# Blocks of one and two chunks, units of one chunk by two batches, and a mixture's first product in tiles of 64 rows

## The chip, the cores and the metric

One core of one Trainium2 chip, all in 32-bit floats. The metric is the time of one execution on the device in microseconds (us), as the median of several executions. Executions fall into a fast and, now and then, a slow state. A ratio is the mean time of one kernel's fast runs over that of the kernel before's fast runs in the same rounds on the same chip, so it isn't quite the ratio of the medians that stand beside it.

Words used throughout: TensorE multiplies matrices, VectorE and ScalarE work elementwise, SyncE and GpSimd here mostly start transfers (DMA). The *clock* is the share of full speed that TensorE was granted, as its profile records it. Names like `pef` or `ph` are those of the tiles that TensorE writes. *Filler* is mixture work that TensorE does while the recurrence waits for something. A *half* is a matmul of the first mixture product with 64 rows instead of 128; two halves on different rows of the array can run at the same time and are then a *pair*.

## The reference

A recurrence over 768 tokens for 4 batches of 8 heads, then a mixture of four experts over all 3072 tokens.

```python
# r, k, v, w, a, b: (4, 8, 768, 40); state: (B, H, 40, 40)
for t in range(S):
    y[:, :, t] = einsum('bhd,bhde->bhe', r_t, state)
    Sa = einsum('bhde,bhe->bhd', state, a_t)
    state = state * w_t[..., None] - einsum('bhd,bhe->bhde', Sa, b_t) + einsum('bhd,bhe->bhde', v_t, k_t)
x = y.transpose(0, 2, 1, 3).reshape(3072, 320)
for e in range(4):                       # w1[e]: 320 x 1024, w2[e]: 1024 x 320
    out += p[:, e:e + 1] * (np.maximum(x @ w1[e], 0) @ w2[e])
```

## The kernel before

The recurrence goes in chunks of 64 tokens. Within a chunk it is a triangular system. It is solved on VectorE's lanes for all heads at once. A block is two chunks of all four batches, and a *unit* is one batch of it. For each block the kernel prepares four units (transposes `pW`, `pNK`, `pKN`, `pA`, `pR`; VectorE's scan, reciprocal and products; `pef`; `pkn`), sends the systems F through DRAM to VectorE's lanes, solves, brings the result back, completes the inverse (`pi`, `px`), and does two dependent steps (`pa` to `py`).

```python
for tb in range(NT):                      # six blocks of 128 tokens
    pairs = [pair(tb, bp) for bp in range(NP)]
    decays(pairs[0], 0)                   # load of W, pW, scan, reciprocal
    for bb in range(B):
        if bb + 1 < B:
            decays(pairs[(bb + 1) // 2], (bb + 1) % 2)
        within(pairs[bb // 2], bb % 2)    # pNK, pKN, pA, pef, pkn, pR
        if bb % 2:
            to_lanes(pairs[bb // 2])      # F -> DRAM -> lanes
    solve()                               # VectorE
    for q in pairs:
        inverse(q)                        # pi, px
    ...                                   # two steps, gather into xT
    if before is not None:
        mixture(tb - 1, before, gate)     # one block behind
    before = xT
mixture(NT - 1, before, gate)
```

The mixture's first product multiplies a depth of 320: two tiles of 128 rows (`w1a`), and one of 64 rows (`w1c`), in which two output tiles run at once.

```python
for f2 in range(NF // 2):
    ph = [mbank("ph") for _ in range(2)]
    for x in ((0, 1) if f2 % 2 == 0 else (1, 0)):
        for d in range(2):
            if x == 1:                    # 64 rows, a pair
                nc.tensor.matmul(out=ph[d][:], lhsT=w1c[half(d), f2, :], rhs=xv[half(d), 2, :], ...)
                continue
            for g in range(2):            # 128 rows
                nc.tensor.matmul(out=ph[d][:], lhsT=w1a[:, g, f * P:(f + 1) * P], rhs=xv[:, g, :], ...)
    ...                                   # relu to hs, on ScalarE
for bb in range(B):
    ...                                   # po: eight 128-row matmuls, scaled and added into osb on VectorE
```

The program states what depends on what. The order of the instructions on each engine is fixed when the kernel is built, by a scheduler that estimates durations: it takes the earliest written instruction that it believes ready. The mixture is written after the recurrence, so it is filler.

Of the kernel before, what the change touches and what calls it, by code (L numbers as in the profile page):

```python
# [14 lines left out]
def kernel(  # L15
# [29 lines left out]

    nc = tc.nc
# [6 lines left out]
    NT = S // P  # L53
    NJ = H // 2
    NP = B // 2
    SL = (0, 64)
    NF = F // P
    NTOK = B * S
# [7 lines left out]

    def bank(name):
        return ps.tile([P, 512], FP32, name=name, tag="bank", bufs=4)
# [4 lines left out]

    ident = const.tile([P, P], FP32, name="ident")
    nc.vector.memset(ident[:], 1.0)
# [3 lines left out]
    )  # L79

    upper = const.tile([P, P], FP32, name="upper")
    nc.vector.memset(upper[:], 1.0)
# [7 lines left out]

    first = const.tile([P, 2 * NJ, L + 1], FP32, name="first")
    nc.vector.memset(first[:], 0.0)
    nc.vector.memset(first[:, :, 0:1], 1.0)



    srcs = {"W": (w, w), "NK": (b, k), "KN": (k, b), "A": (a, a), "R": (r, r)}
    nat = {x: const.tile([P, H, 64], FP32, name=f"nat{x}") for x in srcs}
    for x in srcs:
        nc.vector.memset(nat[x][:, :, D:64], 1.0 if x == "W" else 0.0)  # L100
    w_shift = const.tile([P, 2 * NJ, L + 1], FP32, name="w_shift")
    nc.vector.memset(w_shift[:, :, 0:1], 0.0)
    RV = [const.tile([P, 2, NJ, 2, 64], FP32, name=f"RV{p}_") for p in range(NP)]
    VS = [const.tile([P, 2, NJ, 2, 64], FP32, name=f"VS{p}_") for p in range(NP)]
    XT = [const.tile([P, 2, 2 * NJ, L], FP32, name=f"XT{p}_") for p in range(NP)]
# [12 lines left out]

    def gates():

        gate = const.tile([P, NTOK // P, E], FP32, name="gate")
        total = const.tile([P, NTOK // P], FP32, name="total")
        nc.gpsimd.dma_start(out=gate[:], in_=moe_domain_probs.rearrange("(n p) e -> p n e", p=P))
        nc.vector.reduce_sum(out=total[:], in_=gate[:], axis=AX.X)
        nc.vector.tensor_scalar_add(out=total[:], in0=total[:], scalar1=1e-9)
        nc.vector.reciprocal(out=total[:], in_=total[:])
        nc.vector.tensor_mul(gate[:], gate[:], total[:, :, None].to_broadcast([P, NTOK // P, E]))
        return gate
# [7 lines left out]
    def load(x, tb, bb):  # L136
        t = slice(tb * P, (tb + 1) * P)
        if srcs[x][0] is srcs[x][1]:
            nc.sync.dma_start(out=nat[x][:, :, 0:D], in_=srcs[x][0][bb, :, t, :].rearrange("h t e -> t h e"))
            return  # L140
        for s in range(2):
            nc.sync.dma_start(
                out=nat[x][:].rearrange("p (j s) e -> p j s e", s=2)[:, :, s, 0:D],
                in_=srcs[x][s][bb].rearrange("(j s) t e -> s t j e", s=2)[s, t],
            )
# [11 lines left out]
    class Pair:  # L157
        pass

    def pair(tb, bp):  # L160
        q = Pair()
        q.GI = []
        q.tb, q.bp = tb, bp
        q.G = sb.tile([P, 2, 2 * NJ, L + 1], FP32, name="G", tag="G", bufs=2)
        q.AE = sb.tile([P, 2, 2, 2, NJ, L], FP32, name="AE", tag="AE", bufs=2)
        q.KN = sb.tile([P, 2, 2, NJ, 2, D], FP32, name="KN", tag="KN", bufs=2)
        q.F = sb.tile([P, 2, 2, NJ, L], FP32, name="F", tag="F", bufs=2)
        q.R = sb.tile([P, 2, NJ, P], FP32, name="R", tag="R", bufs=2)
        return q

    def decays(q, i):

        load("W", q.tb, 2 * q.bp + i)
        G = q.G[:, i]
        nc.scalar.copy(
            out=w_shift[:, :, 1:L + 1], in_=turn("W")[:].rearrange("p (c t) -> p c t", t=L),
        )
        nc.vector.tensor_tensor_scan(
            out=G.rearrange("p c t -> p (c t)"), data0=w_shift[:].rearrange("p c t -> p (c t)"),
            data1=first[:].rearrange("p c t -> p (c t)"), initial=0.0, op0=ALU.mult, op1=ALU.add,  # L180
        )
        GI = sb.tile([P, 2 * NJ, L], FP32, name="GI", tag="GI", bufs=2)
        nc.vector.reciprocal(out=GI[:], in_=G[:, :, 1:L + 1])  # L183
        q.GI.append(GI)

    def within(q, i):

        G, GI = q.G[:, i], q.GI[i]
        for x in ("NK", "KN", "A", "R"):
            load(x, q.tb, 2 * q.bp + i)  # L190
        KNT = sb.tile([P, 2 * NJ, 2, L], FP32, name="KNT", tag="KNT", bufs=1)
        for x, name in enumerate(("NK", "KN")):
            nc.vector.tensor_tensor(
                out=KNT[:, :, x, :], in0=turn(name)[:].rearrange("p (m t) -> p m t", t=L), in1=GI[:], op=ALU.mult,
            )
        pa = turn("A")
        for s in range(2):
            nc.vector.tensor_tensor(  # L198
                out=q.AE[half(s), i, s], op=ALU.mult,
                in0=pa[half(s)].rearrange("p (j c t) -> p c j t", j=NJ, c=2),  # L200
                in1=G[half(s), :, 0:L].rearrange("p (j c) t -> p c j t", c=2),
            )

        pef = [bank("pef") for _ in range(2)]
        for c in range(2):
            for j in range(NJ):
                for s in range(2):
# [44 lines left out]
    def square(t, n=Q):  # L252

        return t[:, 0:Q * Q].rearrange("p (a c) -> p a c", c=Q)
# [344 lines left out]
```

## Time and profile before

| | us |
|---|---|
| median of 3 runs | 1418.68 (1415.52 to 1424.13) |
| until the first unit of the second block | 162.6 |
| second block | 235.7 |
| a steady block (blocks 3 to 5) | 219.5 to 221.4 |
| one expert alone | 35.2 |

A block can be read as a sum: its four stages (preparing, waiting for the solve, inverse, steps), in which the recurrence sets the pace and filler is free, and whatever mixture is then left, alone. Before, the stages are 160 us and 59.7 us are left. The lines are in the prediction.

### The profile page before, as it was taken

To read this page: it belongs to the slowest core of one execution; us is meant where nothing else is said; L and a number is where in the kernel's file an instruction comes from. 1 tells how busy PE (TensorE), PEld (TensorE's weight loads), DVE (VectorE), ACT (ScalarE), POOL (GpSimd) and SP (SyncE) were. 2 spreads that over 40 slices of the span, in tenths; PEclk is the share of its full clock that TensorE was granted. 3 is DMA by queue.
4 is the path that set the end of the run, shared out by engine and by line. 5 is a ranking of instruction groups with operands and counts; after the bars stand their busy time and mean duration, and the time that the engine had idled before them with its cause. 6 is when DMAs were issued, how large, how long until landed. Compare 5 with 4: busy or idle time off the path is not lost.

```text
span 1422.5 us, 24433 instructions
## 1 busy us (share of the span) xinstructions
PE 1307.6 (92%) x10592; PEld 870.4 (61%) x10592; DVE 557.3 (39%) x806; ACT 262.0 (18%) x481; POOL 182.7 (13%) x331
## 2 busy tenths in 40 slices
PE   4608899899999999999999999999999999999998
PEld 3608766576557567566568556558555657655555
DVE  8373656232054824045715035625125544200000
ACT  1202131121122131112121113112012213011111
POOL 4000001101201201201200221010220120222220
PEclk8556889999998999999999998999998999999999
DMA  9612454433257433248343356453335342222221
GB/s 147 92 32 42 82 73 101 89 74 81 79 98 113 103 81 80 76 97 122 86 98 62 85 116 93 83 125 60 95 103 74 90 105 62 59 93 76 74 77 50
DMA packets 294217, 121.98 MB, mean 86 GB/s; under 512 B 267184, under 2 KB 277984, under 8 KB 294112
## 3 DMA queue, kind: packets, MB, share of 16 engines
q1 hardware_dynamic: 273696, 57.44, 24.7%
q0 software_dynamic: 20416, 62.99, 16.0%
q8 instruction: 84, 1.38, 0.4%
q14 instruction: 21, 0.17, 0.0%
HBM read 103.07 MB, written 17.30 MB: 85 GB/s over the span
## 4 chain that ended last, share of the span: by engine, by line
PE 74%; DVE 20%; DMA 4%; issue 2%; SPq 0%; ACT 0%; DVEq 0%
PE po L528 24%; PE ph L518 17%; PE ph L511 5%; DVE tmp L279 5%; PE pef L208 5%; DVE GI L183 3%; PE pc L414 3%; PE pkn L226 2%; DVE Xl L283 2%; DVE Y L283 2%; DMA XD<-Tl 2%; PE py L430 2%; PE pa L360 2%; PE py L440 2%; PE pSN L461 2%; PE pt L375 2%
## 5 line engine op out<-in xcount | busy, mean ns | idle before, releaser
L528 PE MATMUL po<-w2s,hs 128*128 128x320 f32 x1536 | 430.9, 438 | 0.0
L528 PEld LDWEIGHTS po<-w2s,hs 128*128 128x128 f32 x1536 | 292.7, 192 | 127.6 <-issue 16.2
L518 PE MATMUL ph<-xT,w1a 128*128 128x512 f32 x768 | 361.2, 610 | 1.5 <-DMA xT<-yD 1.5
L518 PEld LDWEIGHTS ph<-xT,w1a 128*128 128x128 f32 x768 | 139.9, 192 | 172.6 <-issue 168.7
L536 DVE SCALAR_TENSOR_TENSOR osb<-po,gate,osb 128x320 f32<-128x320 f32 x72 | 39.6, 551 | 463.3 <-PE po L528 463.3
L524 ACT ACTIVATE hs<-ph 128x512 f32<-128x512 f32 x192 | 109.6, 596 | 587.0 <-PE ph L511 439.6
L499 POOL DMA_DIRECT2D w1c<-in_moe_w_dram x96 | 53.3, 562 | 794.9 <-PE ph L511 791.2
L511 PE MATMUL ph<-xT,w1c 64*128 64x512 f32 x384 | 111.2, 633 | 0.0
L208 PE MATMUL pef<-AE,KNT 64*128 64x64 f32 x768 | 70.6, 310 | 31.5 <-DVE AE L198 31.5
L208 PEld LDWEIGHTS pef<-AE,KNT 64*128 64x128 f32 x768 | 66.8, 221 | 45.8 <-issue 34.9
L183 DVE RECIPROCAL GI<-G 128x512 f32<-128x512 f32 x24 | 80.3, 3345 | 0.2
L495 POOL DMA_DIRECT2D w1a<-in_moe_w_dram x144 | 74.3, 522 | 39.5 <-PE ph L518 32.5
L321 PE MATMUL pi<-F 32*32 32x32 f32 x768 | 18.7, 199 | 56.8 <-DMA F<-XD 56.8
L511 PEld LDWEIGHTS ph<-xT,w1c 64*128 64x128 f32 x384 | 36.0, 189 | 55.7 <-issue 54.7
L503 POOL DMA_DIRECT2D w2s<-in_moe_w_dram x24 | 22.1, 921 | 366.0 <-PE po L528 365.9
L218 DVE TENSOR_TENSOR AE<-pef,mask 64x512 f32<-64x512 f32 x48 | 33.1, 689 | 72.8 <-ACT F L214 72.0
L467 DVE COPY SN<-pSN 128x512 f32<-128x512 f32 x24 | 16.6, 692 | 109.8 <-PE pSN L461 109.8
L321 PEld LDWEIGHTS pi<-F 32*32 32x32 f32 x768 | 16.1, 115 | 69.2 <-issue 67.4
L414 PE MATMUL pc<-R,VST 64*128 64x64 f32 x768 | 48.5, 276 | 6.0 <-DVE VST L467 5.6
L414 PEld LDWEIGHTS pc<-R,VST 64*128 64x128 f32 x768 | 45.2, 188 | 14.2 <-DVE VST L467 7.1
L214 ACT COPY F<-pef 64x512 f32<-64x512 f32 x48 | 27.8, 580 | 120.3 <-PE pef L208 119.8
L279 DVE TENSOR_TENSOR tmp<-Xl,Gl 128x256 f32<-128x256 f32 (+3 forms) x36 | 45.6, 1266 | 0.6
(108 smaller groups left out, 1134.9 us busy)
## 6 DMA issues: line engine op xcount, KB each, us to landing
w2s<-in_moe_w_dram POOLq DMA_DIRECT2D x24, 1280.0 KB, 7.4
w1a<-in_moe_w_dram POOLq DMA_DIRECT2D x144, 160.0 KB, 3.9
w1c<-in_moe_w_dram POOLq DMA_DIRECT2D x96, 64.0 KB, 2.3
natW<-in_w_dram SPq DMA_DIRECT2D x24, 160.0 KB
natA<-in_a_dram SPq DMA_DIRECT2D x24, 160.0 KB
natR<-in_r_dram SPq DMA_DIRECT2D x24, 160.0 KB
yD<-Yo SPq DMA_DIRECT2D x48, 80.0 KB
out_dram<-osb SPq DMA_DIRECT2D x24, 160.0 KB
```

What stands on the lines that cost most here:

```text
L183: nc.vector.reciprocal(out=GI[:], in_=G[:, :, 1:L + 1])
L208: nc.tensor.matmul(out=pef[s][:, (c * NJ + j) * L:(c * NJ + j + 1) * L], lhsT=KNT[half(s), 2 * j + c].rearrange("p x t -> p (x t)"), rhs=q ...
L279: nc.vector.tensor_tensor(out=m, in0=in0[:, :, None, :].to_broadcast([P, n0, n1, nr]), in1=in1[:, None, :, :].to_broadcast([P, n0, n1, nr] ...
L283: nc.vector.tensor_reduce(out=out, in_=m, axis=AX.X, op=ALU.add, negate=negate)
L414: nc.tensor.matmul(out=pc[s][:, at], lhsT=VST[half(s), i, j * P:(j + 1) * P], rhs=q.R[half(s), i, j, c * L:(c + 1) * L], start=True, stop= ...
L495: nc.gpsimd.dma_start(out=w1a[j * D:(j + 1) * D, s, :], in_=moe_w1[e, h * D:(h + 1) * D, :])
L499: nc.gpsimd.dma_start(out=w1c[SL[d] + s * KR:SL[d] + (s + 1) * KR], in_=moe_w1[e, h * D + P - K0:(h + 1) * D, :].rearrange("r (f d x) -> r ...
L511: nc.tensor.matmul(out=ph[d][:], lhsT=w1c[half(d), f2, :], rhs=xv[half(d), 2, :], start=(f2 % 2 == 1), stop=(f2 % 2 == 0),)
L518: nc.tensor.matmul(out=ph[d][:], lhsT=w1a[:, g, f * P:(f + 1) * P], rhs=xv[:, g, :], start=(f2 % 2 == 0 and g == 0), stop=(f2 % 2 == 1 and ...
L524: nc.scalar.activation(out=hs[-1][:], in_=ph[d][:], func=ACTF.Relu)
L528: nc.tensor.matmul(out=po[:, 0:DM], lhsT=hs[f][:, bb * P:(bb + 1) * P], rhs=w2s[:, f, :], start=(f == 0), stop=(f == NF - 1),)
L536: nc.vector.scalar_tensor_tensor(out=osb[bb][:], in0=po[:, 0:DM], scalar=sc, in1=osb[bb][:], op0=ALU.mult, op1=ALU.add,)
```

## The change

Its intent: a first block of one chunk, so that the mixture begins sooner, and a last block of one chunk, so that little mixture is left at the end; units of one chunk by two batches, which suit both block sizes; and a first product made of pairs alone, with fewer changes of the array's tiling. The diff, cut to its core (renaming, loads, buffers and constants left out):

```diff
-    for tb in range(NT):
-        pairs = [pair(tb, bp) for bp in range(NP)]
+    blocks_of = [[0]] + [[c, c + 1] for c in range(1, NC - 1, 2)] + [[NC - 1]]
+    for cs in blocks_of:
+        units = [Of(c=c, x=x, p=p, ...) for x, c in enumerate(cs) for p in range(NP)]
 ...
     def load(x, u):
-        nc.sync.dma_start(out=nat[x][:, :, 0:D], in_=srcs[x][0][bb, :, t, :]...)
+        for i in range(2):
+            nc.sync.dma_start(out=nat[x][half(i)][:, :, 0:D], in_=...)
 ...
-            w1a = wts.tile([P, 2, F], FP32, name="w1a", tag="w1a", bufs=1)
-            w1c = wts.tile([P, NF // 2, P], FP32, name="w1c", tag="w1c", bufs=1)
+            w1s = wts.tile([P, NK, F // 2], FP32, name="w1s", tag="w1s", bufs=1)
 ...
-                for x in ((0, 1) if f2 % 2 == 0 else (1, 0)):
+                for k_ in range(NK):
                     for d in range(2):
-                        if x == 1:
-                            nc.tensor.matmul(... w1c[half(d), f2, :] ...)
-                            continue
-                        for g in range(2):
-                            nc.tensor.matmul(... w1a[:, g, f * P:(f + 1) * P] ...)
+                        nc.tensor.matmul(
+                            out=ph[d][:, 0:n], lhsT=w1s[half(d), k_, f * P:(f + 1) * P], rhs=xT[half(d), k_, 0:n],
+                            start=(k_ == 0), stop=(k_ == NK - 1),
+                        )
 ...
-            nc.sync.dma_start(out=out[row:row + P, :], in_=osb[bb][:])
+            for i in range(2):
+                nc.sync.dma_start(out=out[row:row + L, :], in_=osb[tt][half(i)])
```

## The prediction

> **What bounds the kernel now.** I read the page first (busy shares, the 40 slices), then the chain of waits, then the busy time in chosen stretches, then TensorE's timeline through one block, then its waits. The kernel has two halves: a recurrence over chunks of 64 tokens and, one block behind it, a mixture of four experts (first product `ph`, second product `po`) that fills TensorE while the recurrence waits.
>
> ```profile
> PE 1307.6 (92%) x10592; PEld 870.4 (61%) x10592; DVE 557.3 (39%) x806; ACT 262.0 (18%) x481; POOL 182.7 (13%) x331
> PE   4608899899999999999999999999999999999998
> PEclk8556889999998999999999998999998999999999
> ```
>
> TensorE is busy nearly everywhere but in the first four slices (36 us each), where it is idle or at a granted clock near half. One steady block (398 to 618 us), cut at its own stages (preparing the units; waiting for the triangular solve; inverse; two steps; mixture alone):
>
> ```profile
> 398.00:453.00 55.00, 52.02 (x302) 35.44 (x301) 33.56 (x33) 16.10 (x31) 7.20 (x13) 0.88 0.73 118
> 453.00:498.80 45.80, 43.16 (x145) 24.89 (x144) 30.48 (x52) 5.34 (x10) 7.23 (x13) 1.00 0.41 98
> 498.80:517.20 18.40, 18.40 (x238) 10.31 (x238) 1.10 (x2) 4.53 (x8) 0.93 (x1) 1.00 0.46 112
> 517.20:558.20 41.00, 40.05 (x904) 35.15 (x903) 22.31 (x39) 10.52 (x21) 0.00 (x0) 1.00 0.29 54
> 558.20:618.00 59.80, 59.80 (x201) 34.57 (x198) 4.55 (x8) 6.84 (x12) 13.45 (x25) 1.00 0.31 85
> ```
>
> The columns are length, then busy us of PE, PEld, DVE, ACT, POOL, then clock, DMA share, GB/s. The first four stages, 160 us, are the recurrence; 60 us are mixture alone. So a block is 220 us. What matters is the second stage. From TensorE's timeline there:
>
> ```profile
> 449.07 2.33 PE L208 MATMUL pef<-AE,KNT 64*128 64x64 f32 x32
> 451.34 1.09 PE L226 MATMUL pkn<-ident,KNT 128*128 128x128 f32 x8
> 453.24 13.62 PE L528 MATMUL po<-w2s,hs 128*128 128x320 f32 x50
> 466.70 3.60 PE L518 MATMUL ph<-xT,w1a 128*128 128x512 f32 x8
> 470.23 1.99 PE L511 MATMUL ph<-xT,w1c 64*128 64x512 f32 x8
> 472.15 7.13 PE L518 MATMUL ph<-xT,w1a 128*128 128x512 f32 x16
> 484.67 11.47 PE L528 MATMUL po<-w2s,hs 128*128 128x320 f32 x42
> 498.77 0.22 PE L321 MATMUL pi<-F 32*32 32x32 f32 x2 [2.64 <-DMA F<-XD]
> ```
>
> From the last `pef` (ends at 451.3) to the first `pi` are 47.4 us: F through DRAM to the lanes, the solve on VectorE, the result back through DRAM. TensorE has just enough mixture in that gap and waits only 2.64 us. The same wait in the whole run, and the path's other two ends:
>
> ```profile
> PE pi L321 <- DMA F<-XD: 56.8, 8, 40.0
> 456.07 0.48 SPq L243 DMA_DIRECT2D Gl<-FD  x1
> 463.07 0.15 DVE L267 TENSOR_TENSOR tmp<-Xl,Gl 128x4 f32<-128x4 f32 x1
> 491.60 0.46 SPq L307 DMA_DIRECT2D XD<-Xl  x1
> ```
>
> 40 us of the wait belong to the first block, which has no mixture. In the first block the solve starts 3.5 us after the issue of Gl (67.93 to 71.39); here it starts after 7.0, since an eviction of `po` stands ahead of it in VectorE's order.
>
> **What the skill says.** Trainium skill, "TensorE: Matmul & The Clock Gate", Part 2: matmuls stay in program order, only weight loads are pulled ahead. So TensorE's built order is fixed, and filler placed after `pi` can't move ahead of it. The trace agrees: it idles 2.64 us before `pi` although `po` matmuls stand right behind.
> Same page, Part 3: matmuls of different row groups run at the same time. The trace agrees: each f32 matmul of the program is two records; the eight 64-row records at 470.23 take 1.92 us until 472.15, while the sixteen 128-row ones take 7.06, so 441 ns each. Eight in pairs are four slots of 427 ns and 0.2 us over.
> "TensorEngine Tiling (Array Packing)", Key Properties: a change of tiling mode drains the array. The trace agrees as to size: that 0.2 us over, and 0.1 to 0.2 at each run of 128-row records beside them.
> First page, Part 1: idling beyond a window of some 3.4 us halves the clock. The trace agrees: after 2 us of waiting at 409 us the clock falls to 0.60 in 412 to 416 us, and it stays near 0.5 from 427 to 436, with small matmuls alone.
>
> **The change part by part.**
> *First product in 64-row tiles.* Before, per expert: 16 full matmuls and 8 half ones, 1278.16 to 1296.12 in the chain of waits, 17.96 us; `po` takes 17.23 (35.2 together). After: 40 half matmuls, two by two, 20 pairs of two slots of 427 ns, 17.1 us, and one entry and exit, 0.3: 17.4. The array does the same work; four mode changes become two. Gain 0.5 us per expert, with 24 experts' worth about 10 us. The count of instructions is 40 for 24.
> *Blocks of 1, 2, 2, 2, 2, 2, 1 chunks.* Seven solves for six. A solve runs on all lanes at once, so half the lanes make it no shorter. The short ends cost two half mixtures of about 17.6 us an expert. Prologue: only two of four units are prepared. The last `pef` then ends near 34.8 instead of 63.7 us (the second unit's group starts at 34.40 and takes 4.37, less 4 for the third unit's scan and reciprocal, 1.2 and 3.3, which no longer stand between): 29 off. One step of 19.6 us off; the half inverse 3 off; 1 on for a split dot product. So 162.6 us (the first transpose of the next block) less 50.6 is 112.
> *Units of one chunk by two batches.* The same transposes, `pef`, `pkn` and steps. Loads become two half-size DMAs each; 18 issues per unit at 0.5 us are 9 us of SyncE, under a unit's 12 to 14 us. Gathers read whole kilobyte rows. Neutral.
> *What the order does.* This is the part that decides it. The instruction order of the changed kernel shows what fills each gap. Between last `pef` and first `pi` of a steady block: `pkn`, one `ph`, `pR`, 6 `ph`, 32 `po`, 26 `ph`. Costs: 1.0, 1.05 (alone: two slots and mode changes), 0.44, 2.8, 17.3, 11.3 (13 pairs): 33.9 us. Before it was 45. The order looks as if a half matmul had been counted at 0.86 us: 33 x 0.86 + 17.2 + 1.4 is 47, just the length of the path. In pairs they take half of that, so the filler runs out.
> The path itself: 47.4, less 3.5 (the solve no longer stands behind evictions), plus 1.65 (three more evictions of 0.55 inside it), plus 0.6 (two products of 2048 split): 46.1. So TensorE idles 46.1 - 33.9, about 12 us, before each `pi`, and 2 us more are lost to the halved clock after.
> The stages of a steady block then: preparing the units about 52 (before 55; 7 us less filler, but its VectorE chain of scan, reciprocal, KNT and AE, about 11.5 us a unit, now bounds it and the clock drops oftener); solve gap 45; inverse 16.5 with the halved clock (before 18.4 with more filler); steps 40.5. Sum 154. The rest of the mixture: 22 `po` x 0.54, then two experts of 34.7: 81. Block 235, for 220.
> Last block: two units 25, gap 45, inverse 10, one step 19, about 100; then 26 `ph` and 32 `po` (28.3) and two experts (69.5); then the half mixture, 4 x 17.6, with about 4 us of waiting for weights (a w2s load lands in 7.4 us and now has only some 8.6 us to hide behind) and 2 at the end.
> Sum: prologue 112; first pair block 162 (8 more than a steady one, as before, where it is 16 longer) and 15 of mixture left, 177; four blocks of 235, 940; last 100 + 98 = 198; tail 76. Together 1503; I say 1500.
> Check by the same sum before: 162.6 + 235.7 (from 162.6 to 398.3) + 4 x 220 + 4 x 35.2 = 1419, which is measured.
>
> **The rivals.**
> (a) *The prologue's 50 us and the 10 us of mode changes are pure gain, and the middle stays TensorE-bound.* For it: 92% busy, and one block less of waiting at the start. Then 1419 - 10 - 50 + about 45 for the extra half block's own stage, filled as well as before: about 1400. Against it: the idle before `pi` follows from fixed order and measured durations.
> (b) *The preparing stage sinks to half clock for most of its length.* With filler of 2.6 us a unit instead of 3.4 to 5, little dense work holds the clock up. At half clock a unit takes some 15 us (the first block's reciprocals start 15.2 us apart). Then that stage is 58 to 62 and the time 1530 to 1545.
> (c) *Pairs do not hold over twenty in a row, or not with 256 columns,* because two weight loads must pass per slot. Against it: in `pef` 30 records with 64 columns take 2.13 us, so 142 ns a pair, under the 213 ns of a 256-column slot. If a quarter of the overlap were lost, the filler would grow but the mixture too (4.3 us an expert, 103 in all, some 20 of it in the gaps): about 1580.
> (d) *The stage is shorter than I take it,* since less filler also shortens inverse and preparation: at 146 us a stage the time is near 1460.
>
> **Range and chances.** The gap is robust; stage lengths are good to some 8 us in five blocks, the prologue to 6. So 1450 to 1540 holds it 8 times in 10. Faster by over 2% (under 1390) needs the gap to be filled: 0.06. Within 2%: 0.10. Slower: 0.84.
>
> **What would show it.** TensorE's wait for F before `pi` at 10 to 14 us a block, 90 to 130 us in all with the prologue's; solve from `pef` to `pi` near 46 us; 40 `ph` in 17 to 17.5 us where they stand alone; mixture beginning near 120 us; PEclk digits below 9 once or twice a block. I am wrong if those waits stay at 2 to 3 us, if the blocks stay at 220 us, or if the first block ends much later than 112 us.

## The result, and the profile after

1615.84 us, median of 4 runs (1598.12 to 1624.76, the longest in the slow state), against 1418.16 of the kernel before beside it; ratio 1.1346, 95% interval 1.1241 to 1.1451. The changed kernel is slower by 198 us, over twice the predicted 80, and outside the range. The page of the profiled run (span 1617.8 us), busy time of the engines, and the clock granted to TensorE in 40 slices of 40.4 us:

```profile
PE 1421.8 (88%) x11680; PEld 967.9 (60%) x11680; DVE 588.9 (36%) x877; ACT 266.3 (16%) x521; POOL 75.4 (5%) x108
...
PEclk9576989978999969899978879997889998789999
```

TensorE is busy 114 us longer than before (1307.6) for the same arithmetic, and idle 81 us longer (196 against 115). The clock row now has a 7 or an 8 in each block, where it had nearly all 9. The steady block from 545.5 us, by the prediction's stages (length; busy PE, PEld, DVE, ACT, POOL; clock; DMA share; GB/s):

```profile
545.50:613.60 68.10, 57.66 (x296) 39.54 (x295) 32.78 (x31) 13.78 (x26) 0.93 (x1) 0.75 0.37 72
613.60:660.70 47.10, 37.45 (x143) 21.21 (x143) 30.88 (x55) 5.70 (x11) 2.28 (x3) 0.86 0.46 99
...
723.60:805.16 81.56, 81.56 (x336) 47.89 (x333) 6.20 (x11) 8.69 (x16) 4.57 (x6) 1.00 0.34 83
```

The first line is what to look at: 68.1 us of preparing, of which TensorE is busy 57.7, at a clock of 0.75. The kernel before, in its steady block from 618 us:

```profile
618.00:671.20 53.20, 50.22 (x290) 34.31 (x288) 32.43 (x31) 14.63 (x28) 7.19 (x13) 0.87 0.72 116
```

So the stage is 15 us longer: half of it is waiting (10.4 us for 3.0), half is work at a lower clock (57.7 for 50.2), though the kernel before had more filler there: 32 `ph` records of 128 rows, 16 halves' records and 12 of `po`, by 0.44, 0.22 and 0.27 us some 21 us, against 66 halves' records, some 15 us. The solve's gap has about the same length as before (47.1 for 47.3), but TensorE is busy only 37.5 us of it. TensorE's timeline (start, length, what; in brackets the wait before it and its releaser):

```profile
545.51 0.60 PE L165 MATMUL pW<-ident,natW 128*128 128x128 f32 x4
546.04 2.85 PE L463 MATMUL ph<-xT,w1s 64*128 64x512 f32 x12
554.55 1.09 PE L165 MATMUL pW<-ident,natW 128*128 128x128 f32 x4 [5.66 <-DMA natW<-in_w_dram]
...
558.13 3.31 PE L463 MATMUL ph<-xT,w1s 64*128 64x512 f32 x12
562.89 2.69 PE L209 MATMUL pef<-AE,KNT 64*128 64x64 f32 x32 [1.46 <-DVE AE L202]
565.52 1.63 PE L229 MATMUL pkn<-ident,KNT 128*128 128x128 f32 x8
567.07 2.07 PE L463 MATMUL ph<-xT,w1s 64*128 64x512 f32 x2
...
578.30 3.86 PE L209 MATMUL pef<-AE,KNT 64*128 64x64 f32 x32 [2.27 <-DVE AE L202]
```

After the second `pW` has waited 5.66 us, a `pW` group takes 1.09 us instead of 0.60, a `pef` group up to 4.16 (at 595.21, not shown) instead of 2.0, and a single half `ph` 2.07: half clock. Three of the four units then wait before `pef`, and the clock falls again. The end of the solve's gap, and one first product standing alone:

```profile
639.62 11.43 PE L463 MATMUL ph<-xT,w1s 64*128 64x512 f32 x52
660.71 0.28 PE L316 MATMUL pi<-F 32*32 32x32 f32 x2 [9.66 <-DMA F<-XD]
```
```profile
510.81 17.44 PE L463 MATMUL ph<-xT,w1s 64*128 64x512 f32 x80
```

The pairs do overlap: 80 records in 17.44 us, as predicted. What TensorE waited for in the whole run (us in all, times, longest):

```profile
PE pi L316 <- DMA F<-XD: 86.2, 9, 38.6
PE pW L165 <- DMA natW<-in_w_dram: 38.7, 8, 5.7
PE pef L209 <- DVE AE L202: 33.0, 18, 6.1
PE pa L366 <- issue: 8.3, 3, 3.9
```

The kernel before had 56.8, 12.0, 31.5 and 1.5 on these lines. The first block, without filler, has some 40 us of the first line in both. The rest is now about 10 us in each steady block (predicted 12), where it was 2 to 3. On the third line the first block, with four units before and two now, has 17.7 us of the old sum and 7.3 of the new; in all other blocks `pef` waits 25.7 us where it waited 13.8. The wait for W was not predicted.

### The profile page after: what moved, and what is told of

Read it like the earlier page. It is cut to its first block, busy times and chain, and to the rows that moved or that the text cites. A ratio compares the mean times of both kernels' runs of the same rounds, so it can differ in the third digit from the quotient of the medians.

```text
span 1617.8 us, 26714 instructions
## 1 busy us (share of the span) xinstructions
PE 1421.8 (88%) x11680; PEld 967.9 (60%) x11680; DVE 588.9 (36%) x877; ACT 266.3 (16%) x521; POOL 75.4 (5%) x108
## 3 DMA queue, kind: packets, MB, share of 16 engines
q8 instruction: 92, 1.51, 0.4%
## 4 chain that ended last, share of the span: by engine, by line
PE 68%; DVE 19%; DMA 8%; SPq 3%; issue 2%; ACT 0%; DVEq 0%; ACTq 0%
PE ph L463 22%; PE po L473 20%; DVE tmp L275 5%; PE pef L209 4%; DVE GI L188 3%; PE pc L405 3%; PE pkn L229 2%; DMA natW<-in_w_dram 2%; DVE Xl L279 2%; PE pSN L338 2%; DVE Y L279 2%; PE pa L366 2%; PE pt L376 2%; PE py L417 1%; DMA XD<-Tl 1%
## 5 line engine op out<-in xcount | busy, mean ns | idle before, releaser
L463 PE MATMUL ph<-xT,w1s 64*128 64x512 f32 (+1 forms) x2240 | 529.2, 574 | 12.8 <-DVE osb L481 9.7
L463 PEld LDWEIGHTS ph<-xT,w1s 64*128 64x128 f32 x2240 | 242.0, 200 | 218.0 <-issue 190.9
L469 ACT ACTIVATE hs<-ph 128x512 f32<-128x512 f32 (+1 forms) x224 | 111.2, 534 | 734.9 <-PE ph L463 734.1
L209 PE MATMUL pef<-AE,KNT 64*128 64x64 f32 x768 | 79.4, 311 | 33.1 <-DVE AE L202 33.0
L209 PEld LDWEIGHTS pef<-AE,KNT 64*128 64x128 f32 x768 | 76.1, 220 | 48.9 <-issue 40.3
L453 POOL DMA_DIRECT2D w1s<-in_moe_w_dram x56 | 37.9, 682 | 961.7 <-PE ph L463 961.7
L165 PE MATMUL pW<-ident,natW 128*128 128x128 f32 x96 | 22.5, 380 | 38.7 <-DMA natW<-in_w_dram 38.7
L275 DVE TENSOR_TENSOR tmp<-Xl,Gl 128x1024 f32<-128x1024 f32 (+5 forms) x49 | 54.2, 1107 | 0.8
L199 DVE TENSOR_TENSOR KNT<-pNK,GI 128x512 f32<-128x512 f32 x24 | 16.5, 690 | 94.9 <-PE pNK L165 94.9
L165 PEld LDWEIGHTS pW<-ident,natW 128*128 128x128 f32 x96 | 16.9, 199 | 44.3 <-issue 38.7
```

The costliest lines, as they stand in the source:

```text
L165: nc.tensor.transpose(out=p[:, j * P:(j + 1) * P], in_=nat[x][:, 2 * j:2 * j + 2, :].rearrange("p h e -> p (h e)"), identity=ident[:],)
L209: nc.tensor.matmul(out=pef[s][:, m * L:(m + 1) * L], lhsT=KNT[half(s), m].rearrange("p x t -> p (x t)"), rhs=u.AE[half(s), s, m, :], start ...
L275: nc.vector.tensor_tensor(out=m, in0=in0[:, :, None, :].to_broadcast([P, n0, n1, nr]), in1=in1[:, None, :, :].to_broadcast([P, n0, n1, nr] ...
L453: nc.gpsimd.dma_start(out=w1s[half(d)], in_=moe_w1[e, :, d * (F // 2):(d + 1) * (F // 2)].rearrange("(k p) f -> p k f", p=64),)
L463: nc.tensor.matmul(out=ph[d][:, 0:n], lhsT=w1s[half(d), k_, f * P:(f + 1) * P], rhs=xT[half(d), k_, 0:n], start=(k_ == 0), stop=(k_ == NK ...
L469: nc.scalar.activation(out=hs[-1][1][:, 0:n], in_=ph[d][:, 0:n], func=ACTF.Relu)
```

## The experiments

All 15 gave the correct result. Medians, and ratios to the kernel before of the same rounds:

| run | first product | filler | us | ratio |
|---|---|---|---|---|
| the change | pairs | as scheduled | 1615.84 | 1.135 |
| full_rows | 128-row | as scheduled | 1433.81 | 1.010 |
| two_chunks | pairs | as scheduled | 1599.69 | 1.126 |
| out_pool | pairs | as scheduled | 1608.22 | 1.134 |
| pairs_before | pairs, in the kernel before | as scheduled | 1566.38 | 1.104 |
| small_before | as before | as scheduled | 1425.41 | 1.004 |
| start_only | pairs | 11 us kept for the start | 1590.43 | (half slow) |
| thin_full | 128-row | by hand, little | 1567.60 | 1.104 |
| thin_pairs | pairs | by hand, little | 1569.28 | 1.107 |
| placed | pairs | by hand, much | 1470.72 | 1.036 |
| placed60 | pairs | the same, more before `pef` | 1421.53 | 1.000 |
| placed60_gap | pairs | the same, more before `pi` | 1405.88 | 0.991 |
| placed_full | 128-row | by hand, much | 1389.91 | 0.977 |
| placed_full_gap | 128-row | the same, more before `pi` | 1374.64 | 0.966 |
| placed_full_two | 128-row, all blocks of two chunks | by hand, much | 1381.64 | 0.972 |
| placed_full_two_gap | 128-row, all blocks of two chunks | more before `pi` | 1351.55 | 0.954 |

The verdicts at 2%: placed_full_gap, placed_full_two and placed_full_two_gap are faster than the kernel before; full_rows, small_before, placed60 and placed60_gap are the same; placed_full is unclear (interval 0.975 to 0.980); start_only has no verdict; the others are slower.

### Which part of the change costs: full_rows, two_chunks, pairs_before, small_before

The theories at the start: (1) filler lost in the solve's gap because of the pairs; (2) the late load of W halves the preparing stage's clock; (3) the small end blocks cost; (4) the pairs themselves are poor filler.

**full_rows.** The change with the first product as before.

```diff
-            w1s = wts.tile([P, NK, F // 2], FP32, name="w1s", tag="w1s", bufs=1)
+            w1a = wts.tile([P, 2, F], FP32, name="w1a", tag="w1a", bufs=1)
+            w1c = wts.tile([P, NF // 2, P], FP32, name="w1c", tag="w1c", bufs=1)
...
-                for k_ in range(NK):
-                    for d in range(2):
-                        ...                      # pairs only
+                for x in ((0, 1) if f % 2 == 0 else (1, 0)):
+                    ...                          # as in the kernel before
```

> The changed kernel with the first mixture product as in the kernel before (128-row tiles for two thirds of the depth, 64-row pairs for the rest). By the order of TensorE's instructions this puts some 45 us of mixture back between the last pef and the first pi of a block, where the changed kernel has 33.9. Theory 1 (the gap's filler was lost because of the pairs, and the idle time lowers the granted clock of the inverse and the steps): the pi wait of about 10 us a steady block falls to 2 or less, the gap stays near 46 us, the inverse returns to 16.5 and the steps to 41, so 8 to 12 us are won in each of 5 pair blocks elsewhere than in the gap, and 1540 to 1570 comes out; the preparing stage stays near 68 us because its W wait is untouched. Theory 2 (the late second half of W halves the clock of the preparing stage) says the same of that stage: still 66 to 70 us. Theory 4 (64-row pairs as filler are themselves what the clock suffers from): the preparing stage too comes back to 54 us and the time falls to 1480 or less. If only the end blocks matter (theory 3): 1600 or more.

1433.81 us. Its steady blocks take 223 to 230 us, their preparing stages 58 to 62, and the two largest waits fall:

```profile
PE pi L316 <- DMA F<-XD: 51.2, 8, 37.3
PE pW L165 <- DMA natW<-in_w_dram: 22.7, 6, 4.5
```

37.3 of the first line's 51.2 us are the first block's. So all the other parts of the change together cost 13 us (interval 1.005 to 1.016), and the pairs cost some 180. Theory 4 alone had named so low a time, but theory 1, read more widely (filler lost in every stage, not only in the gap), says the same. The two are separated further down. Theory 2 had the W wait stay as it was. It fell from 38.7 to 22.7 us although no load of W was moved.

**two_chunks.** Pairs, no small end blocks.

```diff
-    blocks_of = [[0]] + [[c, c + 1] for c in range(1, NC - 1, 2)] + [[NC - 1]]
+    blocks_of = [[c, c + 1] for c in range(0, NC, 2)]
```

> The changed kernel, but with blocks of two chunks throughout: six blocks, five of them steady, no small first and last block. Theory 3 (the extra, seventh preparing and solving stage is what costs): some 1480 or less. Theories 1, 2 and 4 (what costs sits in each steady block): steady blocks stay at 255 to 262 us, five or so of them, prologue some 160, one first block of about 185 less or equal, tail about 140 for the experts alone: 1590 to 1640, within 2% of the changed kernel.

1599.69 us, steady blocks of 253 to 263 us. Theory 3 falls: without the end blocks less than 1% is won (ratio 1.126 for 1.135, and their intervals overlap).

**pairs_before.** The other way round: the kernel before with pairs. The savings of memory that it needed were run alone as a control.

```diff
-            w1a = wts.tile([P, 2, F], FP32, name="w1a", tag="w1a", bufs=1)
-            w1c = wts.tile([P, NF // 2, P], FP32, name="w1c", tag="w1c", bufs=1)
+            w1s = wts.tile([P, NK, F // 2], FP32, name="w1s", tag="w1s", bufs=1)
...
+                for k_ in range(NK):
+                    for d in range(2):
+                        nc.tensor.matmul(out=ph[d][:], lhsT=w1s[half(d), k_, f2 * P:(f2 + 1) * P], rhs=xv[half(d), k_, :], ...)
```

> The kernel before with the first mixture product in tiles of 64 rows and two of its output tiles at once, and nothing else of the change but the savings of memory that this needs. Its order has about 33 us of mixture between the last pef and the first pi instead of 45. Theory 1: each of the five steady blocks gets a pi wait of some 10 us and a lower clock after it, 219.9 to 232 to 238 us, the time 1480 to 1515, so about half of the change's cost; its preparing stage stays near 54 us as one load of W isn't behind two stores. Theory 4: its preparing stage grows too, to 62 or more, and the time is 1520 or more. If the pairs cost nothing (theories 2 and 3 alone): 1405 to 1430.

> The kernel before with only the savings of memory that its version with pairs needed (16 instead of 17 buffers for the hidden layer, a smaller scratch tile with split products): the control for that run. All theories: within 1% of the kernel before, 1410 to 1432. If it is slower than 1440, part of what that run showed is not the pairs'.

The control took 1425.41 us, so the savings cost 0.4%. The pairs took 1566.38, more than theory 1 allowed and in theory 4's range, though the preparing stage (59 to 61 us) grew less than that theory said. A steady block takes 254 us instead of 220. I had expected the difference as idle time in the stages. It is mostly elsewhere: 82.5 us of mixture are left alone at the end of a block instead of 59.7, so 23 us less of it went into the stages, and the stages, which should have become shorter with less to do, grew from 160 to 172 us. The preparing stage and the inverse of the block from 671.7 us:

```profile
671.70:730.80 59.10, 51.53 (x286) 36.19 (x284) 32.62 (x31) 12.54 (x24) 0.93 (x1) 0.74 0.51 88
...
775.70:802.70 27.00, 26.96 (x296) 13.24 (x296) 0.00 (x0) 5.76 (x10) 1.35 (x2) 0.57 0.22 44
...
841.80:924.30 82.50, 82.50 (x337) 48.58 (x337) 6.20 (x11) 8.68 (x16) 4.55 (x6) 1.00 0.32 82
```

Clock 0.74 in the first line and 0.57 in the second, 1.00 in the third, where the same pairs and `po` run alone. So pairs in long runs hold the full clock. Theory 4's cause, if there is one, had to be in the mixing.

### The wait for W: out_pool and start_only

**out_pool.** The output stores move from SyncE to GpSimd, so that no load of W stands behind a store that waits for the last eviction.

```diff
-                nc.sync.dma_start(out=out[row:row + L, :], in_=osb[tt][half(i)])
+                nc.gpsimd.dma_start(out=out[row:row + L, :], in_=osb[tt][half(i)])
```

> The changed kernel with the output stores issued from GpSimd instead of SyncE, so that both halves of the load of W are issued without standing behind stores that wait for the last eviction. Theory 2: the wait of the second pW of a block on natW (5 to 5.7 us each, 38.7 in the run) falls to 1 us or less, TensorE doesn't idle there, and the granted clock of the preparing stage rises from 0.75 to 0.85 or more: stage 52 to 58 instead of 67.8, the time 1616 - 5 x (10 to 16) = 1535 to 1565. If the lower clock has another cause (theory 4 or theory 1), only the wait itself goes: 1616 - 5 x 5.5 = about 1588. If the second half waits anyway for the 1.28 MB load of w2s that is issued at the same moment, nothing changes: 1605 to 1620.

1608.22 us, and the wait is still 35.2 us. The loads and the next wait in its timeline:

```profile
556.62 0.91 POOL L457 DMA_DIRECT2D w2s<-in_moe_w_dram  x1 [2.67 <-PE po L473]
...
556.79 1.28 SPq L156 DMA_DIRECT2D natW<-in_w_dram  x2
...
565.32 1.09 PE L165 MATMUL pW<-ident,natW 128*128 128x128 f32 x4 [5.79 <-DMA natW<-in_w_dram]
```

The two halves of W are issued one behind the other from 556.79, the second some 0.6 us later, and `pW` still waits until 565.3. Beside them lies the 1280 KB load of `w2s`, issued at 556.62, whose landing takes 7.0 us by the page. The third branch of the expectation holds. The Trainium skill says in "DMA: Bandwidth & Descriptors", Issuing engines are not separate DMA queues, that DMAs started by any of these engines run on the same 16 DMA engines and interleave. This run fits it: the stores are out of the way, the `w2s` load is on another engine's queue than that of W, and W is as late. The kernel before loads W in one DMA. That was issued at 618.62, 0.17 us behind its `w2s`, and was in by 621.86, when `pW` started without a wait. So the second DMA of the split load seems to get in among the packets of `w2s`, where the single one got ahead of them; that reading was not tested by itself. This run also has none of the 3 to 4 us stalls named "issue" of the changed kernel (0.6 at most). Its steps are shorter (42.2 us for 44.7, mean of four steady blocks) and its inverse is longer (23.5 for 19.4), so the time is as long; the stalls are not the main cost.

**start_only.** Now the filler itself: the last 11 us of the old block's mixture are kept back and written between the first and the second `pW`. The mixture becomes a generator that yields its own length in tenths of a us, and `fill(n)` writes as much of it at that place.

```diff
         decays(units[0])
+        fill(90)
...
-        if before is not None:
-            mixture(*before)
-        before = (cs, xT)
+        fill(sum(left) - 90)
+        works.append(mixture(cs, xT))
```

> The changed kernel in which only the last 11 us of the mixture of the block before are kept back and stand between the first and the second pW of a block, where the changed kernel has 2 us; everything else of the order stays as the scheduler makes it, with 34 us before pi and small pieces in the preparing stage. If the wait for W (5 to 5.7 us a block) is what starts the half clock of the preparing stage: that wait goes, the clock of the stage rises to 0.85, and 15 us a block go with it: 1530 to 1550. If each shortage of mixture in that stage has its own cost: only the wait itself, some 5 us a block, is won: 1580 to 1600, and the clock after each of the waits for AE before pef stays at 0.5 for about 10 us.

1590.43 us. Two of the four runs were slow; the fast ones took 1566 and 1589, one inside the second branch and one between the two, so the gain is 27 to 50 us and no closer. The wait for W falls from 38.7 to 12.2 us. The preparing stages from 525.7 and 781.7 us keep a clock of 0.78, against 0.75 and 0.73 in the same blocks of the changed kernel (the first steady block has 0.86 here), and the waits for AE before `pef` stay (32.4 us in all). The stage from 525.7 us holds 32 `po` records more, 8.8 us, and is 3.0 us longer, so without them 5.8 shorter: the W wait costs about its own length. Theory 2 falls: it is not what holds the clock down.

### Amount against tiles: thin_full, placed, placed_full

If the amount of filler per stage decides, 128-row tiles with little filler must be slow, and pairs with much must be fast.

**thin_full.** 128-row tiles, filler by hand as scarce as in the changed kernel.

```diff
+        with tc.issue_after(last[0].ins):        # behind the unit's pA
+            fill(34)
         pef = [bank("pef") for _ in range(2)]
...
+        with tc.issue_after(last[0].ins):        # behind the last pef
+            fill(330)
         for q in qs:
             inverse(q)
+        with tc.issue_after(last[0].ins):        # behind the last pi
+            fill(80)
...
+        with tc.issue_after(last[0].ins):        # behind the last py
+            fill(sum(left) - 0)
```

> 128-row tiles in the blocks of the changed kernel, with the mixture held back by order so that each stage gets as much of it as in the changed kernel: 14 us in the preparing stage, 34 between pef and pi, 9 at the inverse, none in the steps. Theory A: as slow as the changed kernel, 1590 to 1640, with pi waits of about 10 us a block and a clock of 0.70 to 0.80 in the preparing stage. Theory B: the pi wait alone, with its clock: 1434 plus 5 x 12 to 15, so 1490 to 1510, and the preparing stage's clock stays at 0.85.

**placed** and **placed_full.** Much filler by hand, with pairs and with 128-row tiles.

```diff
         decays(units[0])
+        fill(90)
...
+        fill(40)
         pef = [bank("pef") for _ in range(2)]
...
             within(u)
+            fill(20)
...
+        fill(430)
         for q in qs:
             inverse(q)
+            fill(35)
```

> The changed kernel with its 64-row pairs, but the mixture of the block before is written between the parts of the recurrence by hand, so that TensorE's order has about 39 us of it in the preparing stage and 46 us between the last pef and the first pi (changed kernel: 15 and 34). Theory A (what costs is only the amount of mixture that the fixed order puts into each stage): the pi wait falls to 2 us or less a block, the clock of all stages to 0.85 or more, and the time is 1380 to 1440, at least as good as with 128-row tiles (1434). Theory B (64-row pairs hold the clock up less well, or slow the small matmuls beside them, in whatever amount): the preparing stage stays below a clock of 0.80 and the time is 1500 or more.

> The same placing by hand, with the first product in 128-row tiles as in the kernel before: the control for the run with pairs. Theory A: within 15 us of the placed pairs, with the pairs some 0.5 us an expert (10 us) better. Theory B: it is 1380 to 1440 while the placed pairs are 80 us or more slower.

thin_full took 1567.60 us: 134 us slower than full_rows and 178 slower than placed_full, with the same tiles and blocks. So little filler alone, without any new pair, costs most of what the change costs. But the time is 22 us below theory A's range, and the loss is not divided as in the changed kernel. The preparing stage was 53 us at a clock of 0.87, not 0.75, although TensorE waited 13 us in it. The loss sat in the gap (46 to 52 us, with waits of 8 to 10 before `pi`), in the inverse (24 to 28 us) and above all in the mixture left alone: 83.3 us a block for 57.8 to 63.1 in full_rows.

placed_full took 1389.91, better than both kernels. placed took 1470.72, 145 us better than the change, but theory A had said 1440 at most, and within 15 us of placed_full. What still separated these two is in one place of each preparing stage. placed first, then placed_full, from TensorE's timelines:

```profile
984.54 4.56 PE L464 MATMUL ph<-xT,w1s 64*128 64x512 f32 x20
990.13 0.40 PE L210 MATMUL pef<-AE,KNT 64*128 64x64 f32 x2 [1.03 <-DVE AE L202]
990.86 1.97 PE L210 MATMUL pef<-AE,KNT 64*128 64x64 f32 x30 [0.32 <-DVE AE L202]
992.76 1.91 PE L230 MATMUL pkn<-ident,KNT 128*128 128x128 f32 x8
```
```profile
945.48 1.98 PE L473 MATMUL ph<-xT,w1a 128*128 128x512 f32 x4
947.45 0.40 PE L210 MATMUL pef<-AE,KNT 64*128 64x64 f32 x2
948.17 1.97 PE L210 MATMUL pef<-AE,KNT 64*128 64x64 f32 x30 [0.32 <-DVE AE L202]
950.07 1.09 PE L230 MATMUL pkn<-ident,KNT 128*128 128x128 f32 x8
```

In placed the piece of `ph` before `pef` lasts 4.56 us (20 records). In placed_full it has three parts, from 941.75 to 947.46, 5.7 us, of which the last is shown. AE comes from VectorE at the same distance in both. So the pairs wait 1.03 and 0.32 us where the other waits 0.32, and from `pkn` on they run at half clock: 1.91 us for what takes 1.09. The clock in placed over the following stretches:

```profile
991.50:993.50 2.00, 2.00 (x27) 1.93 (x25) 0.21 (x1) 0.80 (x2) 0.00 (x0) 0.84 0.51 82
993.50:997.50 4.00, 4.00 (x12) 1.98 (x10) 1.17 (x2) 1.21 (x3) 0.00 (x0) 0.50 0.21 33
997.50:1001.50 4.00, 4.00 (x16) 1.87 (x16) 0.00 (x0) 1.78 (x3) 0.00 (x0) 0.73 0.25 43
```

Here a wait of 1 us is followed by some 8 us at a lower clock. By these shares (0.16 x 2 + 0.50 x 4 + 0.27 x 4) that is 3.4 us of work lost. It doesn't always follow. From 514 us on, placed has these same two waits seven times: after five of them `pkn` takes 1.51 to 1.97 us, after two it keeps its 1.09, as here:

```profile
556.72 1.97 PE L210 MATMUL pef<-AE,KNT 64*128 64x64 f32 x30 [0.32 <-DVE AE L202]
558.62 1.09 PE L230 MATMUL pkn<-ident,KNT 128*128 128x128 f32 x8
```

The wait just before these was 1.03 us, as at 990.13. In thin_full, too, `pkn` kept 1.09 us after two of three waits of 1.70 us. Where TensorE waited 0.32 us at most, as in all units of placed_full from 161 us on and of placed60 from 139 us on, `pkn` never took over 1.10. So nearly all slow units follow a wait (one in placed, at 1033.37 us, follows none that is listed), and what else decides isn't shown.

### What separates pairs from 128-row tiles: placed60, placed60_gap, placed_full_gap, thin_pairs

**placed60** has one more piece before each `pef`; **placed60_gap** and **placed_full_gap** 5 us more before `pi`.

```diff
-        fill(40)
+        fill(60)                                 # placed60, placed60_gap: before pef
...
-        fill(430)
+        fill(480)                                # placed60_gap, placed_full_gap: before pi
```

> The hand-placed pairs with one more piece of 1.7 to 2.6 us of mixture ahead of each unit's first pef, and nothing else. In the run before, 20 ph records lasted 4.56 us there where the 128-row version's pieces lasted 5.86, and TensorE then waited 1.04 and 0.32 us for AE, after which the clock was half for some 10 us in two units of each block; the 128-row version waited 0.32 us and kept its clock. If that small shortage is what still separates the two: the waits of pef go from 19 us to 8 or less, the preparing stage from 70 to 75 us to 62 to 65, and the time from 1471 to 1405 to 1430. If pairs as such weaken the clock: 1455 or more.

> The hand-placed 128-row version with 5 us more of mixture before pi. It still waited 2 to 3.5 us for F there and had a clock of 0.73 at the inverse. If that wait is what lowers it: inverse 19 to 14 us and the wait gone, less some 3 us of it given back where the F has to wait for TensorE: 1365 to 1385. If not: 1385 to 1400.

> The hand-placed pairs with 5 us more of mixture before pi. The pairs' steady blocks were still 7 to 9 us longer than those of the 128-row version; 4 us of it stood in one wait per block of ph for an eviction of po that VectorE does only after the solve. If this wait, from the order of VectorE and not from the pairs, is what is left, the extra mixture moves work but the wait stays: 1405 to 1425. If the pairs were only still short of mixture before pi: 1370 to 1390, as fast as the 128-row version.

placed60 took 1421.53 us, 49 better than placed, inside its range. The waits of `pef` fell from 19.2 to 6.9 us and the preparing stage of the steady blocks from 507 us on to 65 us, at a clock of 1.00. placed_full_gap took 1374.64: no wait before the first `pi` in its last five blocks, inverse 14.4 us (16.5 to 21 in placed_full), clock 1.00 in the stages of a steady block, which takes 205.9 us.

placed60_gap took 1405.88, in its first branch: 31 us behind placed_full_gap. TensorE is busy 1283.2 us in one and 1274.0 in the other, 9 of the 31. The waits, in placed60_gap and in placed_full_gap:

```profile
PE pi L317 <- DMA F<-XD: 58.8, 5, 37.7
PE ph L464 <- DVE osb L487: 22.6, 6, 7.7
PE pW L165 <- DMA natW<-in_w_dram: 15.8, 4, 4.5
```
```profile
PE pi L317 <- DMA F<-XD: 47.7, 5, 37.4
PE pW L165 <- DMA natW<-in_w_dram: 11.1, 3, 4.5
PE pef L210 <- DVE AE L202: 10.5, 11, 6.1
PE ph L465 <- DVE osb L494: 6.7, 2, 5.0
```

By these lines the pairs wait 11 us more before `pi`, 16 more for evictions of `po` and 5 more for W, and 3.5 less before `pef` (7.0 in placed60_gap). The second of these looks like an order again, VectorE's. The timeline of VectorE in placed60_gap, for the gap from 577.5 us, shows the four evictions of `po` together, only after the solve:

```profile
617.79 1.92 DVE L487 SCALAR_TENSOR_TENSOR osb<-po,gate,osb 128x320 f32<-128x320 f32 x4
```

In the same gap of placed_full_gap one of the four comes 3 us before the solve's end and three after it. That this is what the pairs lose was not tested by a run.

**thin_pairs** comes from the other end: thin_full again, differing in the tiles alone (and the finer yields that pairs allow).

```diff
-                for x in ((0, 1) if f % 2 == 0 else (1, 0)):
-                    ...                          # 128-row tiles, as in full_rows
+                for k_ in range(NK):
+                    ...                          # pairs, as in the change
+                    if k_ < NK - 1:
+                        yield 9 * n // 512
```

> The run that held the mixture back with 128-row tiles, again with 64-row pairs in the same places and amounts: one closed piece of 3.5 us ahead of each unit's pef, 34 us before pi, 9 at the inverse, none in the steps, and no single half matmul between pkn and pR. With 128-row tiles the preparing stage took 53 us at a clock of 0.87, although TensorE waited 13 us in it; in the changed kernel, with as much mixture in more and smaller pieces, 68 us at 0.75. If pairs hold the clock up less well than 128-row tiles: preparing stage 62 us or more, clock below 0.80, time 1610 or more. If the shape of the pieces is what matters: 52 to 56 us, clock 0.85 to 0.90, and the time within 15 us of the 128-row run's 1568.

1569.28 us, 1.7 us from the 128-row run. A preparing stage of each, thin_full first:

```profile
537.90:591.00 53.10, 39.72 (x270) 28.99 (x268) 32.58 (x31) 13.20 (x25) 2.17 (x3) 0.87 0.47 91
```
```profile
533.20:589.50 56.30, 42.22 (x294) 31.47 (x293) 32.78 (x31) 13.19 (x25) 0.93 (x1) 0.82 0.46 88
```

Written in the same places, pairs and 128-row tiles take the same time, and TensorE is busy as long (1350.6 and 1351.5 us). The waits are divided otherwise: with pairs 69.4 us before `pi` for 97.1, 31.2 for evictions of `po` for 11.2, and 29.5 before `pef` for 20.0. This shows two things. With little filler the pairs have no cost of their own; with much, the 31 us above remain. And the order counts beside the amount: the changed kernel has as much filler in this stage, also in pairs, but in pieces of 3.3 us or less with single halves between `pkn` and `pR`, and takes 65 to 70 us where one closed piece ahead of each `pef` gives 53 to 56 (clock 0.82 in the one shown, below the 0.85 expected). Which of the two, the longer piece or the missing single halves, does it was not separated.

### Are the small end blocks worth anything: placed_full_two, placed_full_two_gap

```diff
-    blocks_of = [[0]] + [[c, c + 1] for c in range(1, NC - 1, 2)] + [[NC - 1]]
+    blocks_of = [[c, c + 1] for c in range(0, NC, 2)]
```

> The hand-placed 128-row version with two chunks in every block, six blocks without the small first and last one. It tells what the small end blocks are worth once the mixture fills the stages: they save about 50 us before the first mixture begins and cost a seventh stage whose own work is some 70 us less what fills it. If they pay: 1405 or more here; if not: 1375 or less; in between they are neutral.

> The best of both single runs together: 128-row tiles, placed by hand, two chunks in every block (1382) and 5 us more before pi (1375). The additional mixture removed 2 to 3.5 us of waiting and 7 us at the inverse in each of three blocks: 1360 to 1375 if the two add up, 1375 to 1385 if not.

1381.64 and 1351.55 us, against 1389.91 and 1374.64 with the end blocks. In the first pair of runs they are neutral by the expectation (8 us, and the intervals of the two ratios overlap), in the second a loss of 23 us. The second run is the best kernel: 4.6% faster than the kernel before (ratio 0.9536, interval 0.9516 to 0.9556), better than the expected range. Its clock row, and one steady block by stages:

```profile
PEclk9656999999999999999999999999999999999999
```
```profile
578.90:640.00 61.10, 60.31 (x358) 41.32 (x356) 35.06 (x36) 14.40 (x27) 2.88 (x4) 1.00 0.53 110
640.00:693.40 53.40, 53.40 (x176) 28.74 (x174) 31.69 (x56) 9.34 (x17) 3.80 (x5) 1.00 0.48 120
...
746.40:784.80 38.40, 38.40 (x124) 21.70 (x125) 2.89 (x5) 4.56 (x8) 2.88 (x4) 1.00 0.29 92
```

The stages take 168 us, longer than the 160 of the kernel before, but they hold so much mixture that 38.4 us are left instead of 59.7.

## Why the prediction was wrong

By its own terms, from the profiled run (steady block: mean of four):

| term | predicted | measured |
|---|---|---|
| prologue | 112 | 107.4 |
| first pair block | 177 | 184.5 |
| steady block | 235 | 259.8 |
| - preparing | 52 | 67.8 |
| - solve's gap | 45 | 46.4 |
| - inverse | 16.5 | 19.4 |
| - steps | 40.5 | 44.7 |
| - mixture alone | 81 | 81.5 |
| last block | 198 | 208.8 |
| tail | 76 | 77.7 |

The differences add up: -4.6 + 7.5 + 4 x 24.8 + 10.8 + 1.7 is 114.6, which leads from 1503 to the 1617.8 of the span.

**Right.** The direction and its main reason: the built order has 34 us of filler in the gap, TensorE idles about 10 us before each `pi`, and the rest of the mixture, 81 us, stands alone. 40 halves in pairs take 17.4 us. The prologue saves 55 us (162.6 to 107.4; predicted 50.6). None of the rivals (a), (c) and (d) came: the gap wasn't filled, the pairs' overlap wasn't lost (17.44 us), and the stages did not get shorter.

**The step that failed** is "preparing the units about 52". It measured 67.8, and accounts for 16 of the 25 us that a steady block missed by (the prediction ended this stage some 1.7 us after the last `pef`, the table at it, so the miss is rather larger). The prediction took the stage to be bounded by VectorE's chain and subtracted the lost filler. In its place the runs showed this. TensorE waits in the stage, 10.4 us of it, and its clock is low, 0.75: where filler is short by a microsecond or two, TensorE waits, and in most of the traced cases its clock is then near half for some 8 us, so that the small matmuls take up to twice as long. So the stage's busy time grew (57.7 against 50.2 us) with less work in it. The prediction had read just such a fall off the kernel before (2 us of waiting at 409 us, then a clock of 0.60) and allowed some 4 us for it and VectorE's chain together (55, less 7 of filler, but 52). Rival (b) had named just this mechanism, but with 58 to 62 us, and I gave it too little weight. The waits that set it off were not all foreseen. The prediction called the split loads neutral, by SyncE's issue times alone. It did not ask when the second half lands and how much filler covers it: 2.9 us of `ph` in the changed kernel, for 8 us of landing.

**Two smaller terms** have the same direction: steps 44.7 for 40.5, inverse 19.4 for 16.5 (three blocks near 17.2, one of 26.1 at a clock of 0.56). Of the steps' excess of 4.2 us a block, 3.0 are the stalls named "issue" (3.61, 3.94, 3.19 and 1.17 us in the four blocks). Their cause stays open.

**What is shown and what is argued.** Shown: with little filler in the same places, tiles of 64 and 128 rows take the same time (thin_pairs and thin_full, 1.7 us apart). With equal tiles, the order alone, with the amount of filler that it gives each stage, moves the time from 1568 to 1375 (thin_full and placed_full_gap), and with pairs from 1616 to 1406 (the change and placed60_gap). Open: the 31 us between pairs and 128-row tiles with much filler, of which 9 are TensorE's busy time. Argued only: why the order is poor with pairs. The prediction's reading, that a half had been counted at 0.86 us where in a pair it costs 0.43, fits the gap of pairs_before too (33 us of filler for a path of 45), and fits VectorE's late evictions. The scheduler's estimates themselves were not seen.

## What to carry to other kernels

A stage that waits for another engine costs its own length plus the work that was not put into it. So compare, for each stage, the filler that the built order gives it with the wait that it must cover, both in measured durations, before judging a change by what the array does. When instructions begin to overlap that a scheduler may count one by one, look whether it still gives each gap what it needs (here 34 us of 46). If it doesn't, place the filler by hand, in closed pieces just ahead of the wait, and give each piece a microsecond to spare, since here a wait of one microsecond could cost over three more through the clock.

## What the Trainium skill lacked or had wrong

- "TensorE: Matmul & The Clock Gate", Part 1, gives the idle time that lowers the clock as a window of about 3.4 us, and names shorter idles between groups as a second failure without a length. In placed, waits of 1.03 and 0.32 us with 0.40 us of `pef` between them were followed by a lower clock in five of seven cases (0.50 from 993.5 us), and 0.32 us alone never in placed_full. A length for idles beside small matmuls and transposes is what was missing.
- The same part gives the way back as about 3.4 us of sustained work. In pairs_before the clock stayed at 0.50 for over 20 us, with TensorE busy all the time by the profile, at `pi` and `px` of 32 rows and pieces of one to six halves (length, busy PE and the clock as above):

```profile
776.50:780.00 3.50, 3.50 (x9) 1.35 (x6) 0.00 (x0) 0.00 (x0) 0.00 (x0) 0.50 0.69 122
...
794.00:797.50 3.50, 3.50 (x10) 1.36 (x8) 0.00 (x0) 0.00 (x0) 0.00 (x0) 0.50 0.00 0
```

  Whether the clock gate counts such matmuls as busy isn't on the page.
- "TensorEngine Tiling (Array Packing)", Key Properties, says that a change of mode drains the array, without a price. One half `ph` alone (2 records) between 128-row matmuls took 1.12 us at full clock (placed, 559.64 us), for 0.43 a half inside a long run of pairs. Its two records one after the other are 0.85 of that at 427 ns each, so some 0.27 us are left for the two changes, an estimate.
- No page says what a change to row tiling does to an order that a scheduler builds from estimates. Here it cost 141 us in the kernel before (pairs_before 1566 for small_before's 1425), though the first product alone takes 17.4 us an expert in pairs and took 18.0.
